# Larger y transfers and an earlier release of the stores in a transfer-bound x + gamma * y kernel

## The chip, the cores and the metric

The kernel runs on one core of one Trainium2 chip. The metric is the device time of one execution in microseconds (us), as the median of several executions. All times compared here are of fast executions (not more than 1.5% above the fastest of their kernel) unless it is said otherwise. The profile's span runs from the first to the last instruction of one profiled execution, and is about 1.2 to 1.4 us shorter than the time of the same execution.

## The reference

```python
B, S, D = 1024, 16, 512            # all bf16
def reference(x, y, gamma):
    return x + gamma * y           # gamma has D elements
```

Seen as 128 partitions of 128 rows of 512 elements, x, y and out are 128 KB per partition each, 16.78 MB in all. y stays whole in on-chip memory and is overwritten by the result. x has room for only 64 of its 128 rows, so its third and fourth loads must wait until the first and second adds have read the rows that they overwrite.

## The kernel before

Four pieces of 32 rows (32 KB per partition). The SP queue issues the loads, the ACT queue issues gamma and the stores, VectorE (DVE) multiplies and adds. Cut to what the argument touches, with comments added:

```python
PIECES = [32, 32, 32, 32]
X_AT = [0, 32, 0, 32]            # where each x piece lies in the x buffer
X_AFTER = [-1, -1, 0, 1]         # the add after which an x load may be issued
SP = [('x', 0), ('y', 0), ('x', 1), ('y', 1), ('y', 2), ('x', 2), ('y', 3), ('x', 3)]
ACT = [('g',), ('s', 0, 0, 2), ('s', 1, 1, 2), ('s', 2, 2, 2), ('s', 3, 3, 3)]
                                 # ('s', first piece, last piece, the add that it waits for)
...
def _take(sem, n, eng):          # wait for n, then take them off again
    return eng.wait_ge(sem, n).then_inc(sem, -n)
...
for c in range(n):
    yt = y_sb[:, piece(c), :]
    _take(s_y[c], 16, nc.vector)
    nc.vector.tensor_tensor(out=yt, in0=yt, in1=gamma..., op=MULT).then_inc(s_dve, 1)
    _take(s_x[c], 16, nc.vector)
    _take(s_dve, 1, nc.vector)
    nc.vector.tensor_tensor(out=yt, in0=x_tile(c), in1=yt, op=ADD).then_inc(s_add, 1)
```

The names x0 to x3 and y0 to y3 below are these pieces. Products and adds are counted from one: the third product works on piece 2.

## Time and profile before

| | before |
|---|---|
| median time | 120.41 us (120.14 to 120.46) |
| span of the profiled execution (120.87 us) | 119.5 us |
| bytes moved | 50.33 MB |
| share of the 16 transfer engines' time in use | 98.9% |
| VectorE busy | 59% |
| last add ends, last store packet ends | 94.6 us, 119.15 us |

The lines that carry this stand in the prediction. One more view bears on what follows: windows of the trace around the change from loads to stores. Columns: the stretch, its length, busy time of each engine, granted clock, share of the 16 transfer engines in use, GB/s.

```profile
core 0: us, PE busy (x) PEld busy (x) DVE busy (x) POOL busy (x), PEclk, DMA share, GB/s
76.00:83.00 7.00, 0.00 (x0) 0.00 (x0) 7.00 (x2) 0.00 (x0) 1.00 1.04 449
83.00:100.00 17.00, 0.00 (x0) 0.00 (x0) 11.43 (x2) 0.00 (x0) 1.00 1.00 432
```

The loads end at 80.4 us in the first window, and its rate does not fall: the store packets stand ready when the last load packet ends. (A packet counts where it starts, so a short window can show a share slightly above 1.) Below, "packet" means one record of a transfer engine in the trace: here always one partition's row, or a 4-byte semaphore write. A transfer "lands" when the last of its 16 semaphore writes has arrived. The records do not name the engine; what is said of each engine is a count over all packets divided by 16.

### The profile page before, as it was taken

How to read it: one execution, taken by the hardware profiler on the slowest of the kernel's cores; microseconds unless marked ns; L12 is line 12 of the kernel's file. 1: busy time of each engine (PE TensorE's matmuls, PEld its weight loads, DVE VectorE, ACT ScalarE, POOL GpSimd, SP SyncE). 2: the span in 40 equal slices, each digit the busy share in tenths (PEclk: the TensorE clock that was granted, in tenths of full speed). 3: DMA queues.
4: the chain of work that ended last, by engine and by line, in shares of the span. 5: the costliest groups of instructions: out<-in, count | busy, mean ns of one | idle time of the engine just before them, and what ended most of it. 6: DMA issues, size and time to landing. Idle time of an engine off the chain costs nothing. (4 is left out here: it accounts for less than half of the span.)

```text
span 119.5 us, 84 instructions
## 1 busy us (share of the span) xinstructions
PE 0.6 (0%) x1; PEld 0.1 (0%) x1; DVE 70.2 (59%) x10; POOL 0.2 (0%) x4
## 2 busy tenths in 40 slices
PE   0100000000000000000000000000000000000000
PEld 0000000000000000000000000000000000000000
DVE  0100000699999289999999999999999600000000
POOL 0000000000000000000000000000000000000000
DMA  7989898998998989898989999898989898989995
GB/s 208 494 373 504 351 526 351 384 493 351 384 493 351 526 351 526 351 515 362 493 384 471 406 428 450 384 493 351 526 351 526 351 526 351 515 362 471 406 471 230
DMA packets 1730, 50.33 MB, mean 421 GB/s; under 512 B 193, under 2 KB 194, under 8 KB 194
## 3 DMA queue, kind: packets, MB, share of 16 engines
q1 hardware_dynamic: 1152, 33.55, 66.4%
q10 hardware_dynamic: 578, 16.78, 32.5%
HBM read 33.56 MB, written 16.78 MB: 421 GB/s over the span
## 5 line engine op out<-in xcount | busy, mean ns | idle before, releaser
L115 DVE TENSOR_TENSOR y_sb<-y_sb,gamma_sb 128x16384 bf16<-128x16384 bf16 x4 | 34.8, 8688 | 18.4 <-DVEq L22 18.4
L120 DVE TENSOR_TENSOR y_sb<-x_sb,y_sb 128x16384 bf16<-128x16384 bf16 x4 | 34.8, 8692 | 0.6
L109 DVE CAST gamma_sb<-gamma_ps 128x512 bf16<-128x512 f32 x1 | 0.7, 692 | 3.4 <-DVEq L22 3.4
L104 DVE MEMSET ones_row<- 1x128 bf16 x1 | 0.2, 165 | 2.0 <-PEq L38 2.0
L107 PE MATMUL gamma_ps<-gamma_row,ones_row 1*128 1x512 bf16 x1 | 0.6, 580 | 4.8 <-PEq L22 4.8
L107 PEld LDWEIGHTS gamma_ps<-gamma_row,ones_row 1*128 1x128 bf16 x1 | 0.1, 100 | 4.8 <-issue 4.8
L149 POOL MEMSET const-bfloat16-1.0<- 128x1 bf16 x1 | 0.1, 101 | 0.0
L149 POOL MEMSET const-uint8-127<- 128x1 uint8 x1 | 0.1, 101 | 0.0
L149 POOL MEMSET const-float32-0.0<- 128x1 f32 x1 | 0.1, 98 | 0.2 <-issue 0.2
L149 POOL MEMSET const-float32-1.0<- 128x1 f32 x1 | 0.1, 98 | 0.0
## 6 DMA issues: line engine op xcount, KB each, us to landing
x_sb<-in_x_dram SPq DMA_DIRECT2D x4, 4096.0 KB, 21.5
y_sb<-in_y_dram SPq DMA_DIRECT2D x4, 4096.0 KB, 35.4
out_dram<-y_sb ACTq DMA_DIRECT2D x4, 4096.0 KB, 23.8
gamma_row<-in_gamma_dram ACTq DMA_DIRECT2D x1, 1.0 KB
```

The lines of the kernel that those rows point to most:

```text
L104: nc.vector.memset(ones_row, 1.0).then_inc(s_ones, 1)
L107: nc.tensor.matmul(gamma_ps, ones_row, gamma_row, start=True, stop=True).then_inc(s_ps, 1)
L109: nc.vector.tensor_copy(out=gamma_sb, in_=gamma_ps).then_inc(s_dve, 1)
L115: nc.vector.tensor_tensor(out=yt, in0=yt, in1=gamma_sb[:, None, :].to_broadcast([P, PIECES[c], D]), op=MULT).then_inc(s_dve, 1)
L120: nc.vector.tensor_tensor(out=yt, in0=x_tile(c), in1=yt, op=ADD).then_inc(s_add, 1)
L149: nc = _bacc.Bacc("TRN2", target_bir_lowering=False, num_devices=1)
```

## The change

Its intent: fewer, larger transfers for y and for the first half of the result, and stores released somewhat earlier, by a signal ("go") placed behind the third product. The diff, cut to its core:

```diff
-SP = [('x', 0), ('y', 0), ('x', 1), ('y', 1), ('y', 2), ('x', 2), ('y', 3), ('x', 3)]
-ACT = [('g',), ('s', 0, 0, 2), ('s', 1, 1, 2), ('s', 2, 2, 2), ('s', 3, 3, 3)]
+# kind, first row, end row, (x only) place in the x buffer
+SP = [('x', 0, 32, 0), ('y', 0, 64), ('x', 32, 64, 32), ('y', 64, 128), ('x', 64, 96, 0), ('x', 96, 128, 32)]
+ACT = [('g',), ('s', 0, 64), ('s', 64, 96), ('s', 96, 128)]
+DVE = [('m', 0), ('a', 0), ('m', 1), ('a', 1), ('m', 2), ('go',), ('a', 2), ('m', 3), ('a', 3)]
 ...
+            if kind == "s" and not went and ("go",) in DVE:
+                _take(s_go, 1, eng)            # the ACT queue, ahead of the first store
+                went = True
             if need > known:
-                eng.wait_ge(s_add, need + 1)
+                eng.wait_ge(s_add, need)       # a store waits for the adds of its own rows
 ...
+    for kind, *args in DVE:
+        if kind == "go":
+            nc.vector.sem_inc(s_go, 1)
+            continue
```

(The comments are added here.)

More of the change, by code (lines that the diff above doesn't have):

```diff
@@ L6 @@
 PIECES = [32, 32, 32, 32]
-X_AT = [0, 32, 0, 32]
-X_AFTER = [-1, -1, 0, 1]
-SP = [('x', 0), ('y', 0), ('x', 1), ('y', 1), ('y', 2), ('x', 2), ('y', 3), ('x', 3)]
-ACT = [('g',), ('s', 0, 0, 2), ('s', 1, 1, 2), ('s', 2, 2, 2), ('s', 3, 3, 3)]
-EARLY = [('x', 0), ('y', 0), ('g',)]
+SP = [('x', 0, 32, 0), ('y', 0, 64), ('x', 32, 64, 32), ('y', 64, 128), ('x', 64, 96, 0), ('x', 96, 128, 32)]
+ACT = [('g',), ('s', 0, 64), ('s', 64, 96), ('s', 96, 128)]
+EARLY = (2, 1)
+DVE = [('m', 0), ('a', 0), ('m', 1), ('a', 1), ('m', 2), ('go',), ('a', 2), ('m', 3), ('a', 3)]
 MULT, ADD = mybir.AluOpType.mult, mybir.AluOpType.add
@@ L56 @@
     y_sb = nc.alloc_sbuf_tensor("y_sb", [P, rows, D], dt).ap()
-    x_rows = max(a + r for a, r in zip(X_AT, PIECES))
+    x_loads = [w for w in SP + ACT if w[0] == "x"]
+    y_loads = [w for w in SP + ACT if w[0] == "y"]
+    stores = [w for w in SP + ACT if w[0] == "s"]
+    for loads in (x_loads, y_loads, stores):
+        assert sum(w[2] - w[1] for w in loads) == rows
+    x_rows = max(w[3] + w[2] - w[1] for w in x_loads)
     x_sb = nc.alloc_sbuf_tensor("x_sb", [P, x_rows, D], dt).ap()
@@ L62, with meets, pieces_of, x_at @@
     s_gamma, s_ones, s_ps, s_dve = sem("s_gamma"), sem("s_ones"), sem("s_ps"), sem("s_dve")
-    s_x = [sem(f"s_x{c}") for c in range(n)]
-    s_y = [sem(f"s_y{c}") for c in range(n)]
-    s_add, s_end, s_out = sem("s_add"), sem("s_end"), sem("s_out")
-    def piece(a, b=None):
-        return slice(starts[a], starts[(a if b is None else b) + 1])
-    def x_tile(c):
-        return x_sb[:, X_AT[c] : X_AT[c] + PIECES[c], :]
-    early, stores = [], 0
-    def ring(eng, what, known=-1):
-        nonlocal stores
-        for w in what:
-            kind, args = w[0], w[1:]
-            need = X_AFTER[args[0]] if kind == "x" else args[2] if kind == "s" else -1
+    s_load = {w: sem("s_" + "_".join(map(str, w[:2]))) for w in x_loads + y_loads}
+    s_add, s_go, s_end, s_out = sem("s_add"), sem("s_go"), sem("s_end"), sem("s_out")
+    added = [a for kind, *a in DVE if kind == "a"]
+    order = {a[0]: k for k, a in enumerate(added)}
+    def meets(a, b, c, d):
+        return a < d and c < b
+    def pieces_of(a, b):
+        return [c for c in range(n) if meets(starts[c], starts[c + 1], a, b)]
+    def x_at(row):
+        return next(w[3] + row - w[1] for w in x_loads if w[1] <= row < w[2])
+    def frees(w):
+        old = x_loads[: x_loads.index(w)]
+        old = [v for v in old if meets(v[3], v[3] + v[2] - v[1], w[3], w[3] + w[2] - w[1])]
+        return [c for v in old for c in pieces_of(v[1], v[2])]
+    early = []
+    def ring(eng, what, n_early):
+        known, went = 0, False
+        for k, w in enumerate(what):
+            kind = w[0]
+            need = frees(w) if kind == "x" else pieces_of(w[1], w[2]) if kind == "s" else []
+            need = max((order[c] + 1 for c in need), default=0)
+            if kind == "s" and not went and ("go",) in DVE:
+                _take(s_go, 1, eng)
+                went = True
             if need > known:
-                eng.wait_ge(s_add, need + 1)
+                eng.wait_ge(s_add, need)
                 known = need
@@ L86, in ring @@
             elif kind == "x":
-                c = args[0]
-                i = eng.dma_start(out=x_tile(c), in_=xv[:, piece(c), :]).then_inc(s_x[c], 16)
+                to = x_sb[:, w[3] : w[3] + w[2] - w[1], :]
+                i = eng.dma_start(out=to, in_=xv[:, w[1] : w[2], :]).then_inc(s_load[w], 16)
             elif kind == "y":
-                c = args[0]
-                i = eng.dma_start(out=y_sb[:, piece(c), :], in_=yv[:, piece(c), :])
-                i.then_inc(s_y[c], 16)
+                r = slice(w[1], w[2])
+                i = eng.dma_start(out=y_sb[:, r, :], in_=yv[:, r, :]).then_inc(s_load[w], 16)
             else:
-                r = piece(args[0], args[1])
+                r = slice(w[1], w[2])
                 i = eng.dma_start(out=ov[:, r, :], in_=y_sb[:, r, :]).then_inc(s_out, 16)
-                stores += 1
-            if w in EARLY:
+            if k < n_early:
                 early.append(i.ins)
-    ring(nc.sync, SP)
-    ring(nc.scalar, ACT)
+    ring(nc.sync, SP, EARLY[0])
+    ring(nc.scalar, ACT, EARLY[1])
     nc.vector.memset(ones_row, 1.0).then_inc(s_ones, 1)
@@ L110, with need @@
     _take(s_dve, 1, nc.vector)
-    for c in range(n):
-        yt = y_sb[:, piece(c), :]
-        _take(s_y[c], 16, nc.vector)
-        nc.vector.tensor_tensor(
-            out=yt, in0=yt, in1=gamma_sb[:, None, :].to_broadcast([P, PIECES[c], D]), op=MULT
-        ).then_inc(s_dve, 1)
-        _take(s_x[c], 16, nc.vector)
-        _take(s_dve, 1, nc.vector)
-        nc.vector.tensor_tensor(out=yt, in0=x_tile(c), in1=yt, op=ADD).then_inc(s_add, 1)
+    landed, open_mults = set(), 0
+    def need(loads, c):
+        for w in loads:
+            if w not in landed and meets(starts[c], starts[c + 1], w[1], w[2]):
+                _take(s_load[w], 16, nc.vector)
+                landed.add(w)
+    for kind, *args in DVE:
+        if kind == "go":
+            nc.vector.sem_inc(s_go, 1)
+            continue
+        c = args[0]
+        yt = y_sb[:, starts[c] : starts[c + 1], :]
+        if kind == "m":
+            need(y_loads, c)
+            g = gamma_sb[:, None, :].to_broadcast([P, PIECES[c], D])
+            nc.vector.tensor_tensor(out=yt, in0=yt, in1=g, op=MULT).then_inc(s_dve, 1)
+            open_mults += 1
+        else:
+            need(x_loads, c)
+            if open_mults:
+                _take(s_dve, open_mults, nc.vector)
+                open_mults = 0
+            at = x_at(starts[c])
+            xt = x_sb[:, at : at + PIECES[c], :]
+            nc.vector.tensor_tensor(out=yt, in0=xt, in1=yt, op=ADD).then_inc(s_add, 1)
     nc.scalar.sem_inc(s_end, 1)
@@ L125 @@
     _take(s_add, n, nc.sync)
-    _take(s_out, 16 * stores, nc.sync)
+    _take(s_out, 16 * len(stores), nc.sync)
     main = nc.main_func.blocks[0].instructions
```

## The prediction

> **What bounds the kernel now.** I read the page first: how full each engine and the transfers are, slice by slice.
>
> ```profile
> PE 0.6 (0%) x1; PEld 0.1 (0%) x1; DVE 70.2 (59%) x10; POOL 0.2 (0%) x4
> ...
> DMA  7989898998998989898989999898989898989995
> ...
> DMA packets 1730, 50.33 MB, mean 421 GB/s; under 512 B 193, under 2 KB 194, under 8 KB 194
> ...
> q1 hardware_dynamic: 1152, 33.55, 66.4%
> q10 hardware_dynamic: 578, 16.78, 32.5%
> ```
>
> VectorE (DVE) works 59% of the span. The DMA row has 8 or 9 in every slice between the first and the last, and the two queues (q1 the loads, q10 the stores and gamma) occupy 66.4 + 32.5 = 98.9% of the 16 engines' time. The 50.33 MB are x, y and out once each, so no byte can be saved. The kernel is bound by transfers, and the whole question is whether the change makes holes in that row or closes any.
>
> Next the timeline, to see who releases what. Columns: start, duration, engine and line, operation.
>
> ```profile
> 22.06 8.69 DVE L115 TENSOR_TENSOR y_sb<-y_sb,gamma_sb 128x16384 bf16<-128x16384 bf16 x1 [15.81 <-DVEq L22]
> 30.90 8.69 DVE L120 TENSOR_TENSOR y_sb<-x_sb,y_sb 128x16384 bf16<-128x16384 bf16 x1
> 39.62 0.33 SPq L88 DMA_DIRECT2D x_sb<-in_x_dram  x1
> ...
> 42.16 8.69 DVE L115 TENSOR_TENSOR y_sb<-y_sb,gamma_sb 128x16384 bf16<-128x16384 bf16 x1 [2.57 <-DVEq L22]
> ...
> 59.72 0.33 SPq L88 DMA_DIRECT2D x_sb<-in_x_dram  x1
> ...
> 77.17 17.78 ACTq L95 DMA_DIRECT2D out_dram<-y_sb  x4
> 85.88 8.69 DVE L120 TENSOR_TENSOR y_sb<-x_sb,y_sb 128x16384 bf16<-128x16384 bf16 x1
> ```
>
> The third x load is issued when the first add ends (39.6), the fourth when the second ends (59.7), the stores when the third ends (77.17). None of these makes a hole: in the trace's packet records the last load packets end at 80.08 to 80.42 and the store packets follow on the same engines from 80.09 to 80.43, a few ns later. The last store packet ends at 119.15. The landing records of the eight loads (x0, y0, x1, y1, y2, x2, y3, x3) stand at 12.1, 21.9, 32.2, 42.0, 51.7, 61.4, 71.1 and 80.8: one 4 MB transfer each 9.7 to 10.3 us, in issue order. The chain of waits explains only the last add (7.3% of the span) and stops there: it does not follow transfers, so it is no guide here.
>
> Where are the lost microseconds? 1,536 packets of 32 KB, 96 on each engine. Undisturbed packets stand 1,209.5 ns apart (the last engine's 32 store packets run from 80.43 to 119.15, 38.7 us). 96 x 1.2095 = 116.1 us, with 12 semaphore packets some 116.2. The span of 119.5 has beside that: 1.0 us to the first packet, about 0.7 us in the first packets (some 2 us each in place of 1.21), about 0.85 us in packets between 16 and 38 us that took up to 1.9 us for a reason I don't see, and 0.4 us from the last packet to the end. The remaining few tenths are the engines' staggered starts. Nothing of this but the 0.85 us is within the change's reach.
>
> **What the Trainium skill says.** "DMA: Bandwidth & Descriptors", section "Where 436 GB/s comes from", puts the ceiling at 16 ports, 435.2 GB/s. The trace agrees: loads from 42 to 71 us moved 432 GB/s. "Why small descriptors are slow" on the same page gives a fixed cost of about 3 cycles per packet. A 32 KB packet at the page's rate takes 32,768 x 16 / 435.2e9 = 1,204.7 ns, so the measured 1,209.5 leaves 4.8 ns a packet: same size. "Issuing engines are not separate DMA queues" says that loads and stores from different engines interleave on the same 16 engines. In the kernel before they never do: loads end where stores begin, so no number here tells what mixing costs. "VectorE: DVE Perf Modes", the perf-mode tier table, puts a bf16 tensor_tensor at two elements a cycle: 16,384 / 2 / 0.96 = 8,533 ns; the page's 8,688 and 8,692 ns agree with it. The change leaves these alone.
>
> **The change, part by part.** Instructions on VectorE are the same ten in the same order.
>
> *Two y loads of 8 MB in place of four of 4 MB.* Load order becomes x0, y(0,1), x1, y(2,3), x2, x3. If a 64 KB row goes as one packet, each engine has 16 fewer load packets and 2 fewer semaphore packets: 16 x 4.8 + 2 x 6 ns = 0.09 us saved. The price is a late start: the first product needs all 8 MB, so it waits for 12 MB rather than 8 MB. 12 MB landed at 32.17 before; VectorE started 0.13 us after its landing (21.93 to 22.06), so product 0 starts at about 32.3, 10.2 us later. All y of rows 0 to 63 is then here, x1 lands at 42, the second y at 61.4, so VectorE runs without the 2.57 us hole that it had at 42. One pair takes 17.45 us (42.16 to 59.61): add 0 ends at 49.8, add 1 at 67.3, product 2 at 75.9, add 2 at 84.7, product 3 at 93.3, add 3 at 102.1. Before it ended at 94.6.
>
> *What this does to the transfers, deadline by deadline.* x2 waits for add 0 (49.8); the queue holds 24 MB and runs dry at 61.4. Slack 11.6 us. x3 waits for add 1 (67.3); the queue with x2 runs dry at 71.1. Slack 3.8 us, of which issue to first packet takes 1.0 to 1.6 (x0 at the start). Left: over 2 us. Loads end at 80.4 as before. The last store is issued at 102.2; the stores ahead of it (12 MB from 80.1, 9.7 us for 4 MB) keep the engines until 109.2. Slack 7 us. Every wait falls where the engines still have work, so all these delays are hidden.
>
> *Stores of 64, 32 and 32 KB, at the end of the third product.* Rows 0 to 63 are ready at 67.3 and held to 75.9, that is 4.5 us before the loads end; before it was 77.17, 3.2 us ahead of the end. After a delay of 1 to 3 us the store packets should take turns with x3's last packets at about 77 to 79. x3 then lands a few us later than 80.8, perhaps 84; it is needed at 93.3. Total bytes do not change, so the end doesn't move. 8 fewer packets and 1 fewer semaphore packet: 8 x 4.8 + 6 ns = 0.04 us.
>
> *Sum:* 0.09 + 0.04 = 0.13 us saved, nothing added on the transfers' path. The span goes from 119.5 to about 119.4, and 120.41 to about 120.3; I say 120.25.
>
> **Rivals.**
>
> 1. *A hole ahead of x3.* The tightest deadline. If add 1 ended over 2 us later than 67.3, each further us would cost one us. For it: slack fell, from 71.1 - 59.7 = 11.4 us before to 3.8. Against it: VectorE's durations repeat within 10 ns, and the landing of 12 MB varies by tenths. Cost if it came: 0.5 to 2 us, so 120.8 to 122.
> 2. *Mixing is dear.* Loads and stores overlap for some 3 to 6 us, which they never did before. If packets took 10% longer then, this would cost 0.3 to 0.6 us: 120.6 to 120.9. Nothing in the profile speaks for or against it.
> 3. *64 KB rows pay more than I say,* or nothing, if the hardware cuts them into 32 KB packets anyhow. Nothing: 120.4. More: the gap to the skill's ceiling over all 96 packets is only 0.46 us, so not below 119.9 by this road.
> 4. *The slow stretch from 16 to 38 us.* Other rows are read then (y instead of x1). If it goes, 0.85 us are won: 119.5. If it doubles, 121.2. It has no visible owner.
> 5. *VectorE becomes the bound.* It ends at 102.1 and the last 4 MB need about 10 us after it: 112, under 119.5. It would take 7 us more delay. Unlikely.
>
> **Range and chances.** The three runs before spread over 0.32 us. Adding rivals 2 and 4 gives 119.6 to 120.9 around 120.25. Faster by over 2% means below 118.0, which is only 1.8 us above the packets' own 116.2 and the starting costs do not go away: 0.01. Slower by over 2% means above 122.8, which needs a hole of over 2.4 us: 0.02. Within 2%: 0.97.
>
> **What would show it.** Right: the same DMA row without holes; 1730 - 256 - 128 - 48 = 1298 packets if a 64 KB row is one packet; product 0 at about 32.3, no idle VectorE after it, the last add ending near 102; x3 issued near 67.4; stores near 76; store packets among the last load packets; x3 landing later than 80.8. Wrong: a slice near 70 to 72 with a lower DMA share (rival 1), longer packets between 77 and 84 (rival 2), 1,682 packets (no merging), a different sum of long packets before 40 us (rival 4).

## The result, and the profile after

The changed kernel takes 127.56 us (median of 5 runs, 127.38 to 127.68) against 120.41. The ratio is 1.060, 95% interval 1.058 to 1.062. Ratios here and below are the mean time of one kernel's fast runs over that of the other's fast runs of the same rounds, so they are not quite the ratio of the medians. The prediction's range ended at 120.9.

First the page of the changed kernel: the DMA rows and the two queues.

```profile
DMA  9799797796989779779799996999799989964977
GB/s 322 342 498 498 332 664 332 332 539 290 498 363 633 332 332 664 332 332 498 342 488 332 498 394 249 405 405 436 249 384 384 373 363 415 446 270 207 498 332 332
DMA packets 1298, 50.33 MB, mean 398 GB/s; under 512 B 145, under 2 KB 146, under 8 KB 146
...
q1 hardware_dynamic: 864, 33.55, 63.3%
q10 hardware_dynamic: 434, 16.78, 33.2%
```

The 1,298 packets are those predicted: a 64 KB row goes as one packet. But there is a dip to 6 and 4 near the end of the DMA row (slices 36 and 37, 110.6 to 116.9 us): a hole. The timeline shows how it came about.

```profile
31.50 8.69 DVE L145 TENSOR_TENSOR y_sb<-y_sb,gamma_sb 128x16384 bf16<-128x16384 bf16 x1 [25.46 <-DVEq L21]
...
49.06 17.77 SPq L106 DMA_DIRECT2D x_sb<-in_x_dram  x2
...
66.39 8.68 DVE L145 TENSOR_TENSOR y_sb<-y_sb,gamma_sb 128x16384 bf16<-128x16384 bf16 x1
66.50 49.03 ACTq L112 DMA_DIRECT2D out_dram<-y_sb  x3
...
83.83 8.68 DVE L145 TENSOR_TENSOR y_sb<-y_sb,gamma_sb 128x16384 bf16<-128x16384 bf16 x1
106.47 8.69 DVE L154 TENSOR_TENSOR y_sb<-x_sb,y_sb 128x16384 bf16<-128x16384 bf16 x1 [13.96 <-DVEq L21]
```

Read the fourth line against the third: the first store is issued at 66.50 us, when the third product has just *begun*, and not when it ends (75.07). The last line has the consequence: VectorE then stands idle for 13.96 us before the last add, because x3 landed only at 106.2 us (landing records of the trace; 80.8 before). The last store is issued at 115.2 us, when the stores ahead of it have all but run out.

Why did the go signal hold nothing? The page counts no semaphore instructions, but the trace's instruction records have them: VectorE's queue raised "go" at 60.58 us, 0.13 us after it had taken the landing of the second y transfer (60.45) and while the second add was still running (57.78 to 66.47). The signal was placed behind the third product in program order, but this bare semaphore increment did not wait for the product ahead of it to be done. The Trainium skill, "Perfetto Trace Analysis", section "Per-instruction lifecycle", tells the two kinds apart: a compute instruction is pushed into a wait queue, after which the sequencer is free for the next instruction, and signals when its bytes are written; a sequencer-only instruction is executed and signalled by the sequencer at once. This trace agrees: 60.58 us for the increment, 66.39 for the start of the product ahead of it.

Two windows of the changed kernel show where the bandwidth went:

```profile
76.00:100.00 24.00, 0.00 (x0) 0.00 (x0) 16.51 (x2) 0.00 (x0) 1.00 0.97 352
112.00:117.00 5.00, 0.00 (x0) 0.00 (x0) 3.17 (x1) 0.00 (x0) 1.00 0.43 184
```

From 76 to 100 us the engines are in use (0.97) but move only 352 GB/s, against 449 and 432 in the two windows of the kernel before: the packets themselves run longer. From 112 to 117 us they are in use only 0.43 of the time: the hole.

The packet records give the ledger. I call "lengthening" each packet's time over its undisturbed time, summed and divided by the 16 engines. "Idle" is engine time with no packet, likewise over 16. Undisturbed packets are counted at their distance from start to start (1,209.5 ns for 32 KB), since neighbouring records overlap by some 3 ns.

| part of the span | before | after | difference |
|---|---|---|---|
| lengthening of the first packets, until 6 us | 0.74 | 0.57 | -0.17 |
| lengthening from 6 to 40 us | 0.87 | 0.01 | -0.86 |
| lengthening after 40 us | 0.02 | 5.02 | +5.00 |
| idle engines, 70 to 117 us (the hole) | 0.02 | 2.89 | +2.87 |
| undisturbed packets (fewer with 64 KB rows) | 116.18 | 116.00 | -0.18 |
| sum of these | | | +6.66 of +6.8 |

The 5.02 us has two parts. 1.06 of it lies in load packets that started between 66.8 and 71.2 us, before the first store packet (71.76). The other 3.95 lies in later packets, nearly all from 75 us on, while loads and stores take turns; 3.2 of it is in the 64 KB store packets. Only the second part is the long packets that are asked about below: the first came in like size in early releases that lost little (0.6 to 1.2 us in e3, e4, e8 and e9).

### The profile page after: what moved, and what is told of

Its sections match the earlier page's. It is cut to its first block, busy times and chain, and to the rows that moved or that the text cites. A ratio compares the mean times of both kernels' runs of the same rounds, so it can differ in the third digit from the quotient of the medians.

```text
span 126.4 us, 81 instructions
## 1 busy us (share of the span) xinstructions
PE 0.6 (0%) x1; PEld 0.1 (0%) x1; DVE 70.1 (55%) x10; POOL 0.2 (0%) x4
## 2 busy tenths in 40 slices
DMA packets 1298, 50.33 MB, mean 398 GB/s; under 512 B 145, under 2 KB 146, under 8 KB 146
```

## The experiments

"Before" was run again beside every group. Its medians there were 120.37 to 120.68 us. Each run's packets are listed in the two tables at the end of this section. The theories at the start: T, the go held nothing, and the early 64 KB store packets took turns with x3's 32 KB packets and starved it; R1, mixing reads with writes is slow of itself; R3, the 64 KB y loads cost something.

### Is it the go signal? (e1, e2)

`e1_go_held` makes the signal wait for the product; `e2_no_go` leaves it out.

```diff
 e1:        if kind == "go":
+               _take(s_dve, open_mults, nc.vector)   # the third product's own signal
+               open_mults = 0
                nc.vector.sem_inc(s_go, 1)
 e2: -DVE = [..., ('m', 2), ('go',), ('a', 2), ...]
     +DVE = [..., ('m', 2), ('a', 2), ...]
```

> The changed kernel with one wait more: VectorE takes the third product's own semaphore before it raises the go signal, so that the go truly comes at the end of the third product (about 75.1 us) and not at 60.6 us as in the trace of the changed kernel. Theory T (the go held nothing back, the first store ran from 66.5 us, and its 64 KB packets took turns with x3's 32 KB packets, so that x3 landed at 106): the first store is issued near 75.2, x3 lands between 80 and 87, the last add starts without a wait near 92.5, the hole near 112 to 117 is gone, time 119.2 to 120.2 us. Rival R1 (64 KB rows, or reads mixed with writes at all, are slow of themselves): still over 124 us.

> The changed kernel without the go signal at all: the stores wait only for their adds. T: the signal was raised before the second add had ended, so nothing changes: 127.3 to 127.8 us, the first store issued at 66.5. Rival (the go held the stores to some use): more than 1 us different from 127.5.

Without the go the time is 127.58 us: the same as with it. With the go held it is 120.85 us, ratio 1.0037 to the kernel before. The timeline of the kernel with the go held:

```profile
75.36 26.59 ACTq L112 DMA_DIRECT2D out_dram<-y_sb  x3
75.45 8.69 DVE L156 TENSOR_TENSOR y_sb<-x_sb,y_sb 128x16384 bf16<-128x16384 bf16 x1 [0.35 <-DVEq L21]
84.06 8.68 DVE L147 TENSOR_TENSOR y_sb<-y_sb,gamma_sb 128x16384 bf16<-128x16384 bf16 x1
92.89 8.69 DVE L156 TENSOR_TENSOR y_sb<-x_sb,y_sb 128x16384 bf16<-128x16384 bf16 x1
```

Holding costs VectorE 0.35 us once. The store goes at 75.36, x3 lands at 83.1, the last add follows without a wait, and no hole is left. So nearly the whole loss hangs on the release, and 64 KB rows are not slow of themselves, which R1 and R3 had as their strong forms. My 119.2 to 120.2 was a little low: there was 0.83 us of lengthening, 0.54 of it in load packets between the stores' issue and their first packet. That first packet came at 79.82 us, 4.5 us after the issue, when the last of x3's data packets had already started (78.94). So x3's data never took turns with the stores here. Only its last semaphore writes waited behind a 64 KB packet, until 82.2 to 82.7 us.

### Early release with equal packets (e3, e4)

`e3_split_store` cuts the first store in two of 32 KB; `e4_before_early` is the kernel before with its first two stores released by the second add.

```diff
 e3: -ACT = [('g',), ('s', 0, 64), ('s', 64, 96), ('s', 96, 128)]
     +ACT = [('g',), ('s', 0, 32), ('s', 32, 64), ('s', 64, 96), ('s', 96, 128)]
 e4: -ACT = [('g',), ('s', 0, 0, 2), ('s', 1, 1, 2), ...]
     +ACT = [('g',), ('s', 0, 0, 1), ('s', 1, 1, 1), ...]
```

> The changed kernel, early release as it is, but the first store as two of 32 KB per partition: store packets are now as large as x3's, so x3 gets half of each engine in place of a third. T: x3's 8 packets an engine need about 8 x 2.43 us in turns and some 10 to 15% for mixing, from 71.7: landing at 92 to 95 and not 106; the last add starts at 92.5 to 95.5, the hole at 112 to 117 closes, and what is left of the loss is the slower packets while reads and writes mix: 120.5 to 123 us. Rival R1 (mixing costs the whole of it, whatever the packet size): 126 us or more. Rival R3 (only the y loads of 64 KB cost): 127.5.

> The kernel before, all 32 KB, but its first two stores released at the end of the second add (59.7 us) in place of the third (77.17). T: y3 and x3 are both still queued then and get half of each engine: y3 lands near 84 in place of 71, x3 near 105 in place of 81, the last add ends near 114, and mixing makes packets longer: 123 to 127 us. Rival R3 (the loss is the 64 KB rows'): 120.4 as before.

121.22 and 121.04 us. For e3 that is in the range, but the run is not clean: with two stores the first needs only the first add, so it went at 60.71, released by the go; here the signal did act. e4 missed my range (123 to 127). x3 landed at 99.1, 18 us later than before, and it still cost only 0.5%, because the stores ahead of the last one kept the engines in work until the last add had ended (108.1 us). Nor were packets long in turns: both runs show 1.04 us of lengthening after 40 us, nearly all of it before the first store packet. **Mixing reads and writes at 32 KB is free but for its start**, so R1 falls.

### Size and moment apart (e5, e8, e9)

`e5_store64_before` is e4 with one 64 KB store in place of two. `e8_split_66` is e3 with both stores held to the second add (66.5 us, the changed kernel's moment), and `e9_store16_66` the same in four stores of 16 KB.

```diff
 e5: +ACT = [('g',), ('s', 0, 1, 1), ('s', 2, 2, 2), ('s', 3, 3, 3)]
 e8: +ACT = [('g',), ('s', 0, 32), ('s', 32, 64), ...]
     +            need = max(need, 2) if kind == "s" else need
 e9: as e8, +ACT = [('g',), ('s', 0, 16), ('s', 16, 32), ('s', 32, 48), ('s', 48, 64), ...]
```

> The kernel before, its loads all 32 KB, with the first two stores made one of 64 KB per partition and released at the end of the second add (59 us): the run with two 32 KB stores at that moment took 121.0. Theory T2 (loads and stores take turns packet by packet, so 64 KB store packets leave 32 KB load packets a third of each engine, and unequal packets in turns also run longer): y3 lands near 88 in place of 78, x3 near 110 in place of 97, the last add ends near 119 and a hole opens ahead of the last store: 128 to 133 us. Rival R3 (the y loads of 64 KB are needed for the loss): 121 to 122.

> As the run with the first store split in two of 32 KB, but both released at the end of the second add (66.5 us) as in the changed kernel: there the first half went at 60.7, which that run's verdict did not separate. T2: x3 has half of each engine from about 71: it lands at 89 to 93 (106 with 64 KB packets), the last add starts without a wait or under 1 us of it, no hole; packets run at full speed but for some 0.8 to 1 us when the stores start: 120.7 to 121.5 us. Rival (the moment of release, not the packet size, made the difference): 125 or more.

> The changed kernel with rows 0 to 63 stored in four pieces of 16 KB per partition, all released at the end of the second add (66.5 us). T2 (turns packet by packet): x3's 32 KB packets now get two thirds of each engine: 8 x (1.21 + 0.61) = 14.6 us from about 71.5, so x3 lands at 85 to 88 (measured 91 with 32 KB store packets, 106 with 64 KB). No wait before the last add. Time 120.7 to 121.5, the start of the stores costing its 0.8 to 1 us. Rival (the engines share by bytes and not by turns): x3 lands at 91 again.

| first stores, released at 66.5 us | x3 lands | time |
|---|---|---|
| 16 KB packets (e9) | 85.8 us | 121.11 us |
| 32 KB packets (e8) | 90.8 us | 121.29 us |
| 64 KB packets (the changed kernel) | 106.2 us | 127.56 us |

In all three, seven of each engine's eight x3 packets were left when the first store packet started (71.1 to 71.8 us). One store packet to one load packet gives 7 x (1.21 + 0.61) = 12.7 us, 7 x 2.43 = 17.0 us and 7 x 3.63 = 25.4 us, that is 84, 89 and 97 us, for x3's last data packet; its semaphore writes wait for one more turn, and it landed 1.0, 1.6 and 2.8 us after the end of its data. The first two fit (the data ended at 84.8 and 89.3). The third falls some 6 us short of the measured 103.5: there the packets were long as well. The queues take turns by packets, not by bytes. This is what the Trainium skill, "DMA: Bandwidth & Descriptors", section "Queues, rings and completion order", says of arbitration, and the order of the packet records agrees with it.

e5 took 130.45 us (130.29 without a slow run of 132.2), so a loss of this kind does not need 64 KB y loads, and R3 falls as the cause of the whole. Here nearly all packets ran at full speed (1.54 us of lengthening, 0.7 of it at the start of the stores, before the first store packet), and nearly the whole loss is the hole: x3 landed at 109.2 us, the last add ended at 118.1, and the engines stood idle for 9.2 us.

### Releasing later (e6, e7)

`e6_release_77` splits the third add into 8 and 24 rows and releases the stores after the 8; `e7_after_add2` releases them at the end of the third add, as the kernel before does.

```diff
 e6: +  nc.vector.tensor_tensor(out=yt[:, :8, :], in0=x_sb[:, at : at + 8, :], in1=yt[:, :8, :], op=ADD).then_inc(s_go, 1)
     +  # then rows 8 to 31; the ('go',) entry is left out
 e7: +            need = max(need, 3) if kind == "s" else need      # and no ('go',)
```

> The changed kernel with the stores released when the first quarter of the third add is done (about 77.6 us, the moment at which the kernel before releases them; the add is split in 8 and 24 rows). T2: the store packets start just as the last load packets end, so no turn is shared and no packet is lengthened; the fewer packets of the 64 KB rows are all that is left: 119.9 to 120.5 us, at or 0.1 to 0.3 below the kernel before, and 0.3 to 0.9 below the run with the go held at 75. Rival (64 KB rows cost something of themselves): 120.7 or more.

> The changed kernel with all stores released at the end of the third add (83.9 us), which is where the kernel before releases its own: the y loads alone are changed in effect. The loads end near 80.3, so the engines are empty until the first store packet, some 1.6 to 3 us after the issue: a hole of 5 to 6.5 us, time 124.5 to 126.5 us. If the hole is smaller, the delay from issue to first packet is smaller than the kernel before made it look.

e7 took 125.54 us, as expected; two windows of it show the price of the larger y transfers alone, a later VectorE and hence a hole where the loads have ended and the stores are not yet there:

```profile
80.00:85.00 5.00, 0.00 (x0) 0.00 (x0) 5.00 (x2) 0.00 (x0) 1.00 0.50 210
85.00:90.00 5.00, 0.00 (x0) 0.00 (x0) 5.00 (x1) 0.00 (x0) 1.00 0.97 419
```

The engines were idle for 5.4 us there. This is what an earlier release was to avoid. The first store packet started 0.9 us after its issue (83.89 to 84.76); my 1.6 to 3 us was read from queues that still had work. In the releases up to 75.4 us, beside running loads, it was 3.0 to 5.4 us (5.3 in the changed kernel, 4.5 in e1).

e6 took 120.70 us, ratio 1.0022 with an interval of 0.9998 to 1.0046: level with the kernel before, slightly outside what I expected, and at the 120.7 that I had given to the rival of 64 KB rows that cost something of themselves. So a cost of a few tenths of a microsecond is not excluded. It is the best form of the change that I found, and it does not beat the kernel before.

### Why were the packets long? (e10 to e18)

> The changed kernel with the 64 KB store released about 2.2 us later, when a first quarter of the third product is done (68.7 us). Two readings of the long packets (64 KB stores of 2.9 to 3.0 us in place of 2.42, from 76 to 100 us, which cost 4.9 us in the changed kernel and did not come in the kernel with 32 KB y loads and a 64 KB store at 59 us). L1, they come with x3's packets beside a 64 KB store: long again, 125 to 127.5 us, x3 at 101 to 105. L2, an accident of how the 16 engines' turns stand to each other: gone or much smaller, x3 near 97 to 99, the hole small, 121 to 123.5 us.

> The kernel before, its loads all 32 KB, with its first two stores made one of 64 KB per partition, released at the end of the third product (about 68 us), held for truly, so that it meets x3 alone as in the changed kernel. L1: packets of 2.9 to 3.0 us again, x3 lands near 104 to 106, 126 to 128 us. L2 or a cause in the y loads of 64 KB (L3): store packets of 2.42, x3 lands near 100 to 102, hole of 1 to 2 us before the last store, 122 to 124 us. In both x3 lands over 15 us later than in the kernel before (80.8), as T2 says.

`e10_release_69` releases the 64 KB store after a first quarter of the third product, 2.4 us later than the changed kernel (the product is split in 8 and 24 rows, and the first part raises the go on completion). `e11_y32_store64_68` is the kernel before with one 64 KB store, released by a held go after the third product (67.77 us). They took 121.11 and 120.84 us; e11 is faster than either reading had it, and x3 landed earlier in both than foreseen (95.2 and 97.9 us). The same window of the changed kernel, of e10 and of e11, in this order, each in a fence of its own:

```profile
76.00:91.00 15.00, 0.00 (x0) 0.00 (x0) 15.00 (x2) 0.00 (x0) 1.00 0.96 345
```

```profile
76.00:91.00 15.00, 0.00 (x0) 0.00 (x0) 15.00 (x2) 0.00 (x0) 1.00 1.03 448
```

```profile
76.00:91.00 15.00, 0.00 (x0) 0.00 (x0) 9.14 (x2) 0.00 (x0) 1.00 1.01 437
```

The same 64 KB store packets take turns with the same x3 packets, and move 448 and 437 GB/s instead of 345. In e10 not one 64 KB packet was long, x3 landed at 95.2, and there was no hole. So **64 KB packets in turns with 32 KB packets are not slow as such**, and 2.4 us decide over 6.4 us of time.

Next, addresses and order:

```diff
 e12 x3_late:      the SP queue waits for the first 8 rows of the third product before it issues x3; the store stays at 66.5
 e13 swap:         third and fourth pieces exchanged, so x3's turn reads rows 64 to 95 instead
 e14 other_rows:   +out=ov[:, (w[1] + 64) % 128 : ..., :]     stores go 64 rows further round: wrong result on purpose
 e15 release_68:   as e10, 4 rows instead of 8
 e16 release_67:   as e10, 1 row instead of 8
 e17 x3_late_67:   as e12, 1 row instead of 8
 e18 halves:       x3 as two transfers, partitions 64 to 127, then 0 to 63
```

> The changed kernel with its 64 KB store released at 66.5 as it is, but x3 issued about 2.2 us later (at the first quarter of the third product, 68.7 us), so that the store is level with or ahead of x3 and not one packet behind it. L2 (the long packets belong to one special standing of the turns: in the changed kernel each engine had sent one x3 packet before its first store packet; with two before it, none was long): no long packets, x3 near 99 to 101, time 120.8 to 122.5. L1 (any turn-taking of x3 with a 64 KB store): already refuted by the run released at 69; it would say 127.

> The changed kernel with its third and fourth pieces exchanged (rows 96 to 127 are loaded, computed and stored before rows 64 to 95): every issue, size, turn and time the same, only that the load which takes turns with the 64 KB store now reads rows 64 to 95 of HBM. A (the long packets come of where the rows read and the rows written lie to each other in HBM): packets change clearly, gone or different, 121 to 124 us. B (they come of the order and timing of packets alone): the same, 127.0 to 127.9 us.

> The changed kernel with its stores written 64 rows further round in out (rows 0 to 63 go to rows 64 to 127 and the other way; the result is wrong on purpose): sizes, order and times as they are, only the address written moves against the address read. A: packets change clearly, 121 to 124 us. B: the same, 127.0 to 127.9.

> The changed kernel with the 64 KB store released about 1.2 us later, when an eighth of the third product is done (67.6 us), between the changed kernel (66.5, one x3 packet ahead, long packets) and the run released at 69 (two ahead, none). If one packet is still ahead and L2 is the order of packets: long, 126.5 to 127.8. If two are ahead: 120.8 to 121.5. If one is ahead and the packets are not long, the order alone is not the cause and the exact phase is.

> The changed kernel with the 64 KB store issued some 0.4 us after x3 (one row of the third product is done first) in place of at the same moment. P1 (the long packets need one x3 packet, not two, ahead of each engine's first store packet): one is still ahead, packets are long, 126.5 to 128 us. P2 (they need the two issues at the same moment): gone, 121 to 123.5. A mixture of fast and slow runs, as the run at 68 gave, would say that the exact phase decides.

> The changed kernel with x3 issued some 0.4 us after the 64 KB store in place of at the same moment; the store stays at 66.5. P1: if one x3 packet is still ahead of the store packets, long, 126.5 to 128 us; if none, as the run with x3 at 68.7 (122.4 to 123.7). P2: 122 to 124 whatever the order.

> The changed kernel with x3 loaded in two transfers, partitions 64 to 127 first and 0 to 63 after, 32 KB packets as before, so that an engine's load packet and its neighbouring store packet no longer belong to the same partition; releases as they are, one x3 packet should still be ahead of the first store packet. Q1 (the long packets come of a load and a store that follow each other in the same partition): gone or much fewer, 121 to 124 us. Q2 (only the count of packets ahead matters): still long, 126.5 to 128 us.

Moving the rows read or written (e13, e14) changed nothing: 127.81 and 127.71 us with packets as long (e14's result is wrong, as intended). So it was not the HBM rows tried. Order comes close to an answer. "Ahead" is the number of x3 packets that had started before the first store packet, divided by the 16 engines; "64 KB packet" is the mean over the whole first store.

| run | x3 issued, store issued | ahead | 64 KB packet | lengthening after 40 us | x3 lands | hole | time |
|---|---|---|---|---|---|---|---|
| e12 | 68.8, 66.5 | 0 | 2,418 ns | 1.1 us | 101.5 us | 2.1 us | 123.21 us |
| e17 | 66.8, 66.4 | 0 | 2,428 ns | 0.4 us | 99.6 us | 1.0 us | 121.1 and 121.3 (two more 123.1 and 123.5) |
| changed | 66.5, 66.5 | 1 | 2,812 ns | 5.0 us | 106.2 us | 2.9 us | 127.56 us |
| e2 | 66.6, 66.6 | 1 | 2,777 ns | 5.1 us | 106.1 us | 2.8 us | 127.58 us |
| e13 | 66.5, 66.5 | 1 | 2,789 ns | 5.2 us | 106.1 us | 2.6 us | 127.81 us |
| e14 | 66.5, 66.5 | 1 | 2,736 ns | 4.8 us | 106.1 us | 2.9 us | 127.71 us |
| e16 | 66.5, 66.9 | 1 | 2,818 ns | 5.3 us | 106.3 us | 2.8 us | 127.69 us |
| e15 | 66.5, 67.7 | 2 | 2,442 ns | 1.0 us | 99.6 us | 0.5 us | 122.6 to 123.0 (one more 127.5) |
| e10 | 66.6, 68.9 | 3 | 2,418 ns | 0.7 us | 95.2 us | none | 121.11 us |

In every kernel of this table with exactly one packet ahead the packets were long, in all 21 of its executions by their times (126.9 to 128.1 us); with none, two or three ahead, the profiled packets were not. e16 also shows that it isn't the common moment of the two issues. e12 and e15 (ratios 1.0225 and 1.0187 to the kernel before) count as unclear at the 2% threshold, and both are above what I expected (120.8 to 122.5 us, and 120.8 to 121.5 with two ahead). e15 jumped to 127.5 us in one execution of four, and e18 had none ahead and yet the longest packets of all (8.3 us of lengthening, 32 KB packets of about 2.0 us while mixed, 130.39 us). Q1 supposes that in the changed kernel neighbouring load and store packets belong to the same partition, which the records do not show. e18 also missed its own premise of one packet ahead, and two half-partition transfers may change which partitions an engine serves, so it cannot tell my Q1 from another cause; beside e12 and e17 it does refute Q2's "only the count matters". **What makes the packets long stays open.** Shown is that it depends on how loads and 64 KB stores stand to each other in their turns, to about a microsecond, and that equal 32 KB packets and 16 KB store packets with one packet ahead (e8, e9) did not have it. One rival is untested: no run had 32 KB y loads with one x3 packet ahead of a 64 KB store, so the long packets may still need the 64 KB y loads (e5 and e11 had other orders).

The remaining runs:

| run | first store packet | lengthening after 40 us | x3 lands | last add ends | hole | time |
|---|---|---|---|---|---|---|
| before | 80.1 us | 0.0 us | 80.8 us | 94.6 us | none | 120.41 us |
| e1 | 79.8 us | 0.8 us | 83.1 us | 101.6 us | none | 120.85 us |
| e3 | 65.4 us | 1.0 us | 96.4 us | 105.3 us | none | 121.22 us |
| e4 | 63.6 us | 1.0 us | 99.1 us | 108.1 us | none | 121.04 us |
| e5 | 63.0 us | 1.5 us | 109.2 us | 118.1 us | 9.2 us | 130.45 us |
| e6 | 79.2 us | 0.6 us | 80.5 us | 101.5 us | none | 120.70 us |
| e7 | 84.8 us | 0.4 us | 80.3 us | 101.3 us | 5.4 us | 125.54 us |
| e8 | 71.8 us | 1.3 us | 90.8 us | 101.3 us | none | 121.29 us |
| e9 | 71.1 us | 0.7 us | 85.8 us | 101.4 us | none | 121.11 us |
| e11 | 72.6 us | 1.0 us | 97.9 us | 106.8 us | none | 120.84 us |
| e18 | 69.6 us | 8.3 us | 109.5 us | 118.4 us | 2.9 us | 130.39 us |

Both tables together give the rule of the hole ahead of the last store (e7's hole is another, ahead of the first): where the last add ended by 108.1 us there was none, from 108.5 on there was one (0.5 us in e15, 1.0 at 108.6 in e17, 2.1 at 110.4 in e12, 9.2 at 118.1 in e5). The prediction's deadline of 109.2 us for the last store was right to within a microsecond, for packets at full speed.

## Why the prediction was wrong, point by point

**What bounds the kernel: right.** 6.66 of the 6.8 us of difference is found again as longer packets or idle transfer engines.

**The step that failed** is, in its words, "Rows 0 to 63 are ready at 67.3 and held to 75.9". They were not held: the increment was raised at 60.58 us, and the store went at 66.50, with the second add. Of the 7.1 us lost this cost 6.7, the difference to e1. The other issues up to that moment came within about 1 us of their predicted times. The order of instructions on VectorE was read as an order of completion, and the rest of the estimate was built on that. With the step made true (e1) the kernel took 120.85 us, at the upper end of the range and 0.6 above the 120.25 named, and the last add ended at 101.6 ("near 102"). That x3 landed at 83.1 us ("perhaps 84") was luck: the delay from issue to first packet was 4.5 us and not "1 to 3", no data packet of x3 took turns, and only its semaphore writes came late. That the release made the loss is shown, by e1 and e2 together; why 4.0 us of it came as long packets is not.

**Rival 2, "Mixing is dear", was mis-sized.** It had 0.3 to 0.6 us for 10% longer packets over 3 to 6 us. With the store at 66.5 us mixing lasted from 71.8 to 103.5 us and its packets cost 4.0 us, with 1.1 before the first store packet and 2.9 of hole beside it. But the prediction's premise was also too simple: in most standings of the turns mixing costs only 0.4 to 1.5 us altogether, most of it before the first store packet.

**"x3 then lands a few us later" missed the share of a turn.** A 64 KB packet against a 32 KB packet leaves the load a third of the engine, which for seven packets is 25 us and not a few. This alone would have been hidden: e10 and e11 had it with x3 at 95 to 98 us and lost 0.2 to 0.4%.

**Rival 1 (a hole ahead of x3) did not come**, the deadline of x3's issue held: 66.5 us against a queue that ran until 70. **Rival 3** was right in its limit: one packet per 64 KB row, 116.18 to 116.00 us. **Rival 4**, the slow stretch from 16 to 38 us, was no property of the kernel: e4, e5 and e11 begin with the same loads and had 0.02 to 0.04 us of it. It seems to have belonged to the one profiled execution (120.87 us against a median of 120.41). The prediction's "up to 1.9 us" is misread: the longest packet there took 1.42 us; the sum of 0.85 is right. **Rival 5** (VectorE becomes the bound) was dismissed as needing 7 us more of delay; the last add came 13 us later than foreseen, so it did take part, through x3.

**The saving of 0.13 us never showed.** Its 4.8 ns a packet is an estimate, the measured distance less a time at the skill's ceiling; e1 gives 4.0 ns (64 KB packets stand 2,415 ns apart, two of 32 KB 2,419), and no run shows the 3 cycles it is compared with. e1 and e6 have it in the packet count, and give it back where the stores start beside running loads (0.5 us of lengthening there in e1 and 0.4 in e6; 0.0 in the kernel before, whose stores start as the loads end).

## What to carry to other kernels

Check a signal's moment, not its place: an increment that stands alone behind a compute instruction may be raised before that instruction has begun (here 5.8 us before); tie it to the instruction's completion, or make the queue wait for that completion first. Where two queues share the transfer engines they take turns by packets, so a larger row takes a larger share: keep the rows of a store no larger than those of a load that somebody still waits for, or hold the store back until that load is nearly done. And in a kernel whose engines are full, a late load costs nothing until the last store comes later than the engines run dry; work that deadline out, and ask what would have to go wrong to miss it.

## What the Trainium skill lacked or had wrong

- "DMA: Bandwidth & Descriptors" describes turns between queues by packets, but not what unequal packets do to the shares: a 32 KB load beside stores of 16, 32 and 64 KB rows landed at 85.8, 90.8 and 106.2 us. It speaks of a packet as several descriptors; in these traces one record is one whole row, up to 64 KB, and the turns went by single records.
- No page has the long packets: 64 KB store packets of 2.74 to 2.82 us on average in place of 2.42, in turns with 32 KB loads, with a loss of about 4 us, present or absent by a microsecond of timing. Their cause is open.
- No page has the start of a store stream beside running loads: load packets between the stores' issue and their first packet were lengthened, by 0.2 us (e17) to 1.2 us (e8, e16) in the early releases, and the first store packet came 3.0 to 5.4 us after its issue.
